# Attention products of a cached decode kernel in four column tiles: V as the moving operand, the sums folded by one fp32 product

## The chip, the cores and the metric

The kernel runs on one core of a Trainium2 chip. The metric is the device time of one execution in microseconds. TensorE (PE) multiplies, with its weight loads shown separately (PEld); VectorE (DVE), ScalarE (ACT) and GpSimd (POOL) do the rest of the arithmetic; SyncE (SP) issues the data transfers, which 16 DMA engines carry out.

## The reference

Eight sequences decode one token each through two identical layers. A layer is layer norm, attention over a cache of 8192 keys with 32 query heads sharing 8 key/value heads, a residual, layer norm, a SiLU feed-forward of width 1792, and a residual. Both layers read the same caches and the same weights.

```
def _A_ref(x, k_cache, v_cache, wq, wo):       # x [8, 1, 512]
    q = (x @ wq).reshape(B, Sq, 32, 128).transpose(0, 2, 1, 3)
    k = jnp.repeat(k_cache, 4, axis=1)         # caches [8, 8, 8192, 128], bf16
    v = jnp.repeat(v_cache, 4, axis=1)
    p = softmax(einsum("bhqd,bhkd->bhqk", q, k) * 128 ** -0.5)
    o = einsum("bhqk,bhkd->bhqd", p, v)
    return o.transpose(0, 2, 1, 3).reshape(B, Sq, 4096) @ wo

x = x + _A_ref(layernorm(x), k_cache, v_cache, wq, wo)
x = x + silu(layernorm(x) @ w1) @ w2
(the same two lines once more)
```

K and V of one pair of a sequence and a key/value head are 2 MB each, of all pairs 268 MB.

## The kernel before

**Tasks.** A task is one layer, one sequence b and one key/value head g: its four query heads against 8192 keys and values. There are 128 tasks. `make_tasks` orders them so that the two layers interleave: of each sequence, the keys of the last five heads stay in SBUF after layer 0 ("kept") and serve layer 1 as well, so that the five layer-1 tasks on them load V alone. The other tasks load K and V. In the steady part a round of fifteen tasks per sequence has five tasks of layer 0 whose keys are kept, five that load everything, and five of layer 1 on kept keys.

**Slots and loads.** `ARENA` has 27 slots of 512 KB. A task's K is four slots and its V four slots. `plan_loads` orders all loads by the position at which they are needed and gives each a slot that an earlier load has left; `issue` (L357) has SP issue the transfer after waiting for the last reader of that slot. Loads therefore run ahead only as far as slots come free.

**Positions.** The main loop (L770) runs over positions p, eight to a task. At each odd position `emit_s` multiplies one K slot and `emit_pv` one V slot of a task 14 positions behind (LP). In between come the pieces of the softmax of the task just scored (`soft`: maximum at phase 0, shift and exponential at 2, sum at 4, transposes at 5, reciprocal at 7), pieces of the `chain` (the dense part of a sequence between its layers: output projection, residual, layer norm, feed-forward, query projection) and the part of the output projection of one head group (`add_heads`). 22 positions after a task's first, `emit_norm` (L561) scales its output. Each engine works strictly in the order in which these calls emit its instructions; waits are semaphores that `op` derives from named resources.

**The attention of a task, in TensorE's terms.** A product is a weight load and a matmul. Column tiles are groups of 32 columns of the array whose results land in 32 partitions of PSUM each.
- `emit_t` (L444): DVE transposes a K slot in place in 32x32 blocks of 4-byte words.
- `emit_q` (L463): four products with the selection matrix `pick` (128 columns of weights, 4 moving columns) spread the query into `QSp`; DVE writes it to `QB` at L466.
- `emit_s` (L481): 16 products per K slot, already in four column tiles: 32 columns of `QB` as weights, 128 columns of K moving, four products accumulated in each tile of `SCp`.
- `softmax_max` (L491), `softmax_shift` (L501): the row maxima, spread out on a diagonal, are multiplied by a 128x128 matrix of ones in fp32, which gives every partition all maxima; DVE takes the smallest negated one (L504, L507).
- `softmax_exp` (L511): ScalarE's exponential from `SCp` to `P`; it reads the bank in order and writes with a step of four elements.
- `emit_pt` (L530): four transposes of 128x128 blocks of P by TensorE; DVE copies the used columns to `PT` (L534).
- `emit_pv` (L554): 16 products per V slot over the full array: 128 columns of V as weights, moving the four probability columns, each repeated 12 times (PVN), so that the four heads' outputs accumulate along the 48 columns of `OTp` over all 64 chunks of a task.
- `emit_norm` (L568): DVE multiplies every twelfth column by the reciprocal sum.

Of the kernel before, what the change touches and what calls it, by code (L numbers as in the profile page):

```python
# [27 lines left out]
KB = 512  # L28
QUAD = 32
FAR = 1e38  # L30
PVN = 12
CW = 32
SETTLE = 2

# [174 lines left out]
def _build(ctx, nc, A_x, A_k_cache, A_v_cache, A_wq, A_wo, B_w1, B_w2, out):  # L209
# [39 lines left out]
    def chunk(slot, c):  # L249
        o = slot * SLOT + c * 128  # L250
        return ARENA[:, o:o + 128]
# [19 lines left out]
    assert NGRAN == NQ and NPART * QUAD == DH  # L271
    QB = [sb([128, NPART, QUAD], BF16, "QB") for _ in range(NQB)]
    own_q = sb([128, NQ], FP32, "own_q")
    pick = sb([128, NPART, 128], BF16, "pick")
# [16 lines left out]
    ones = sb([128, 128], FP32, "ones")  # L291
    hm = sb([128, REP], FP32, "hm")
    real = sb([128, 1], FP32, "real")
    far = sb([128, NQ * USED], FP32, "far")
# [72 lines left out]
    with nc.Block() as block:  # L367

        @block.sync
        def _(sync_eng):  # L370
# [12 lines left out]
            for n in range(NQB):  # L383
# [12 lines left out]
            for i in range(NPART):  # L396
                op(dve, lambda i=i: dve.tensor_copy(
                    pick[:, i, :].rearrange("p (a r) -> p a r", a=NQ),
                    ident[:, i // 2 * 2 * QUAD:(i // 2 + 1) * 2 * QUAD].rearrange("p (r e) -> p e r", e=2)[:, i % 2]
                    .unsqueeze(1).to_broadcast([128, NQ, QUAD])),  # L400
                   reads=["ident"], writes=["pick"])
# [51 lines left out]
            def emit_q(ti):  # L453
                layer, b, g = tasks[ti]
                if layer == 0:
                    q, rq = QT1[:, b * HQ + g * REP:b * HQ + (g + 1) * REP], f"QT1_{b}"
                else:
                    q, rq = QT2[b % 2][:, g * REP:(g + 1) * REP], f"QT2_{b % 2}"
                n = ti % NQB
                steps = []  # L460
                for i in range(NPART):
                    at = (n * NPART + i) * REP
                    steps.append(lambda i=i, at=at: pe.matmul(  # L463
                        QSp[:, at:at + REP], pick[:, i, :], q, start=True, stop=True))
                mm_group(steps, reads=["pick", rq], writes=[f"QS{n}"])
                op(dve, lambda: dve.tensor_tensor(  # L466
                    QB[n][:, :, 0:USED].rearrange("p i (r a) -> p i r a", a=NQ),
                    QSp[:, n * NPART * REP:(n + 1) * NPART * REP].rearrange("p (i r) -> p i r", r=REP).unsqueeze(3)
                    .to_broadcast([128, NPART, REP, NQ]),
                    own_q[:, :].unsqueeze(1).unsqueeze(1).to_broadcast([128, NPART, REP, NQ]), ALU.mult),  # L470
                   reads=[f"QS{n}", "own_q"], writes=[f"QB{n}"])

            def emit_s(i):
                ti = i // GPT
                b, g, k, _h = where(i)
                slot = k_slot[(b, g, k)]
                bank, qn = ti % NSCP, ti % NQB
                keys = ARENA[:, slot * SLOT:(slot + 1) * SLOT].rearrange(
                    "p (t x h j e) -> p t h e x j", t=NQ, x=CPB, h=PAIRS, e=2)
                steps = [  # L480
                    lambda n=n, t=t: pe.matmul(  # L481
                        SCp[bank][t * QUAD:(t + 1) * QUAD, k * 128:(k + 1) * 128], QB[qn][:, n, :],
                        keys[:, t, n // 2, n % 2], start=(n == 0), stop=(n == NPART - 1),
                    )
                    for n in range(NPART) for t in range(NQ)
                ]
                mm_group(steps, reads=[r_half(slot, 0), r_half(slot, 1), f"QB{qn}"], writes=[f"SC{bank}"])
# [9 lines left out]

            def softmax_shift(ti):
                ob = ti % 2
                every = OTp[ob][:, 0:NQ * USED]  # L500
                mm_group([lambda: pe.matmul(every, ones[:, :], spread[:, :], start=True, stop=True)],  # L501
                         reads=["ones", "spread"], writes=[f"OT{ob}"])

                op(dve, lambda: dve.scalar_tensor_tensor(  # L504
                    own[:, :], every, real[:, 0:1], far[:, :], op0=ALU.mult, op1=ALU.add),
                   reads=[f"OT{ob}", "real", "far"], writes=["own"])
                op(dve, lambda: dve.tensor_reduce(shift[:, :], own[:, :], AX.X, ALU.min), reads=["own"], writes=["shift"])  # L507

            def softmax_exp(ti):
                bank, st = ti % NSCP, ti % NST  # L510
                op(act, lambda: act.activation(  # L511
                    P[:, :].rearrange("p (x j k) -> p k x j", x=CPB, k=NGRAN),
                    SCp[bank][:, :].rearrange("p (k x j) -> p k x j", k=NGRAN, x=CPB), ACT.Exp, bias=shift[:, 0:1], scale=SM_SCALE, accum_out=rs[st][:, :]),
                   reads=[f"SC{bank}", "shift"], writes=["P", f"rs{st}"])

            def softmax_sum(ti):
# [7 lines left out]
            def emit_pt(ti):  # L524
                pb = ti % NPT
                tb = evacs[0] % NTP
                evacs[0] += 1
                tpv = TPp[tb][:, 0:KB].rearrange("p (c q) -> p c q", q=128)
                steps = [
                    lambda c=c: pe.transpose(tpv[:, c, :], P[:, c * 128:(c + 1) * 128], ident[:, :])  # L530
                    for c in range(CPB)
                ]
                mm_group(steps, reads=["P", "ident"], writes=[f"TP{tb}"])
                op(dve, lambda: dve.tensor_copy(  # L534
                    PT[pb][:, :, :].rearrange("p x (c q) -> p x c q", q=USED),
                    tpv.rearrange("p x (c q) -> p x c q", q=QUAD)[:, :, :, 0:USED]),
                   reads=[f"TP{tb}"], writes=[f"PT{pb}"])
# [5 lines left out]
            def emit_pv(i):  # L543
                ti = i // GPT
                b, g, k, h = where(i)
                slot = v_slot[(b, g, k)]
                ob, pb = ti % 2, ti % NPT
                pv = PT[pb][:, :, :].rearrange("p x (c r k) -> p x c k r", c=NQ, k=NGRAN)
                otp = OTp[ob][:, 0:REP * PVN].rearrange("p (r n) -> p r n", n=PVN)
                steps = []  # L550
                for c in range(GRP):
                    cc = (i % GPT) * GRP + c
                    steps.append(
                        lambda c=c, cc=cc: pe.matmul(  # L554
                            otp, chunk(slot, h * GRP + c), pv[:, cc % CPB, cc // CPB % NQ, k, :].unsqueeze(2).to_broadcast([128, REP, PVN]),
                            start=(cc == 0), stop=(cc == NCH - 1),
                        )
                    )
                mm_group(steps, reads=[r_half(slot, h), f"PT{pb}"], writes=[f"OT{ob}"])

            def emit_norm(ti):  # L561
                layer, b, g = tasks[ti]
                ob, st = ti % 2, ti % NST
                if layer == 0:
                    dst, rd = at1[b % 3][:, g * REP:(g + 1) * REP], f"at1_{b % 3}"
                else:
                    dst, rd = at2[:, g * REP:(g + 1) * REP, b], f"QT1_{b}"
                op(dve, lambda: dve.tensor_tensor(dst, OTp[ob][:, 0:REP * PVN:PVN], rcp[st][:, :], ALU.mult),  # L568
                   reads=[f"OT{ob}", f"rcp{st}"], writes=[rd])

            def ln_stages(xv, rx, n):
# [198 lines left out]
            for p in range(NG + LP + GPT + 1):  # L770
# [25 lines left out]
                done = p - LP - GPT  # L796
                if done >= 0 and done % GPT == 0 and done // GPT < ntask:
                    tj = done // GPT
                    emit_norm(tj)
                    layer, b, _g = tasks[tj]  # L800
                    if layer == 0:
                        heads[b].append(_g)
                    elif b == B - 1:
                        heads[B].append(_g)
                    if layer == 0 and tj == last0[b]:
                        assert not chain and turn[0] == b
                        chain.extend([lambda b=b: add_heads(b)] * (HKV - summed[b]) + chain_of(b))
                        chain_b[0] = b
                        turn[0] = b + 1
# [49 lines left out]
```

## Time and profile before

Three runs: median 1195.72 us (1193.56 to 1196.29).

| of the profiled execution | value |
|---|---|
| its time | 1198.79 us |
| its span, first to last instruction | 1197.1 us |
| TensorE's mean granted clock | 0.663 of full speed |
| chain that ended last, by engine | DMA 40%, PE 31%, DVE 15%, issue 9%, SP's queue 3%, ACT 2% |
| V loads: number, size, median from issue to landing | 512, 512 KB, 10.3 us |
| K loads | 352, 512 KB, 14.5 us |
| PV products L554: matmuls, busy | 8192, 381.1 us |
| score products L481 | 8192, 287.0 us |
| shift products L501 (two rows to one fp32 product) | 256, 75.4 us |
| transposes L530 | 512, 68.8 us |
| query spread L463 | 512, 32.5 us |
| exponential L511: number, mean | 128, 1409 ns |
| key transposes L444 on DVE: number, mean | 352, 1236 ns |

How to read it: a busy time is the union of an engine's instruction spans; the ends of matmuls are modelled, so products that run side by side in column tiles show up in the union, not in the mean of one. The chain follows the end of the program back from step to step; "issue" in it, and in the waits, is time in which an engine waited for nothing that the profile shows. The DMA queue named "instruction" carries program code, the one named "hardware_dynamic" the data.

### The profile page before, as it was taken

To read this page: it belongs to the slowest core of one execution; us is meant where nothing else is said; L and a number is where in the kernel's file an instruction comes from. 1 tells how busy PE (TensorE), PEld (TensorE's weight loads), DVE (VectorE), ACT (ScalarE), POOL (GpSimd) and SP (SyncE) were. 2 spreads that over 40 slices of the span, in tenths; PEclk is the share of its full clock that TensorE was granted. 3 is DMA by queue.
4 is the path that set the end of the run, shared out by engine and by line. 5 is a ranking of instruction groups with operands and counts; after the bars stand their busy time and mean duration, and the time that the engine had idled before them with its cause. 6 is when DMAs were issued, how large, how long until landed. Compare 5 with 4: busy or idle time off the path is not lost.

```text
span 1197.1 us, 46189 instructions
## 1 busy us (share of the span) xinstructions
PE 839.0 (70%) x20984; PEld 673.4 (56%) x20984; DVE 736.1 (61%) x1830; ACT 183.5 (15%) x266; POOL 70.8 (6%) x172
## 2 busy tenths in 40 slices
PE   1636677767776677767777778777776777677785
PEld 1435566556655566556665566556665656555564
DVE  3736763767456673867457763867376755768464
ACT  0101112111111012111111111111111111111111
POOL 0000000000000000000000000000000000000000
PEclk9955568555765577655866586756775587657765
DMA  9999999999999999999999999999999999999994
GB/s 368 385 396 397 399 355 408 407 394 395 393 408 407 368 389 401 408 404 395 389 408 408 388 397 409 407 402 395 393 407 403 399 393 408 407 392 386 402 408 165
DMA packets 131619, 468.06 MB, mean 391 GB/s; under 512 B 13904, under 2 KB 19808, under 8 KB 130912
## 3 DMA queue, kind: packets, MB, share of 16 engines
q1 hardware_dynamic: 131424, 465.12, 99.1%
q8 instruction: 164, 2.69, 0.9%
q14 instruction: 31, 0.25, 0.1%
HBM read 465.05 MB, written 0.01 MB: 388 GB/s over the span
## 4 chain that ended last, share of the span: by engine, by line
DMA 40%; PE 31%; DVE 15%; issue 9%; SPq 3%; ACT 2%; POOL 0%; POOLq 0%; ACTq 0%; DVEq 0%
DMA arena<-in_A_v_cache_dram 37%; PE OTp L554 14%; PE SCp L481 8%; DVE arena L444 7%; SPq L339 3%; DMA arena<-in_A_k_cache_dram 3%; PE MISC L634 3%; PE OTp L501 2%; PE TPp L530 2%; ACT P L511 2%; DVE rowmax L491 1%; DVE PT L534 1%; PE MISC L652 1%; DVE tr L607 1%; DVE spread L493 1%
## 5 line engine op out<-in xcount | busy, mean ns | idle before, releaser
L554 PE MATMUL OTp<-PT,arena 128*128 128x48 bf16 x8192 | 381.1, 205 | 227.6 <-DMA arena<-in_A_v_cache_dram 182.1
L444 DVE STREAM_TRANSPOSE arena<-arena 128x1024 int32<-128x1024 int32 x352 | 434.9, 1236 | 115.9 <-DMA arena<-in_A_k_cache_dram 115.2
L554 PEld LDWEIGHTS OTp<-PT,arena 128*128 128x128 bf16 x8192 | 316.9, 110 | 331.5 <-DMA arena<-in_A_v_cache_dram 242.6
L511 ACT ACTIVATE P<-SCp,shift 128x512 bf16<-128x512 f32 x128 | 180.3, 1409 | 930.6 <-DVE shift L507 651.5
L481 PE MATMUL SCp<-arena,QB 128*32 128x128 bf16 x8192 | 287.0, 275 | 37.3 <-issue 29.0
L481 PEld LDWEIGHTS SCp<-arena,QB 128*32 128x32 bf16 x8192 | 161.4, 115 | 84.1 <-issue 48.6
L521 POOL PARTITION_ALL_REDUCE ssa<-ssm x128 | 55.6, 435 | 996.0 <-DVE ssm L518 970.8
L534 DVE COPY PT<-TPp 128x256 bf16<-128x256 bf16 x128 | 37.3, 291 | 103.6 <-PE TPp L530 101.8
L501 PE MATMUL OTp<-spread,ones 128*128 128x64 f32 x256 | 75.4, 389 | 25.9 <-DVE spread L493 22.7
L491 DVE TENSOR_REDUCE rowmax<-SCp 128x1 f32<-128x512 f32 x128 | 84.8, 663 | 11.5 <-PE SCp L481 10.3
L530 PE MATMUL TPp<-ident,P 128*128 128x128 bf16 x512 | 68.8, 278 | 13.7 <-ACT P L511 9.6
L504 DVE SCALAR_TENSOR_TENSOR own<-OTp,real,far 128x64 f32<-128x64 f32 x128 | 32.9, 257 | 71.7 <-PE OTp L501 71.7
L501 PEld LDWEIGHTS OTp<-spread,ones 128*128 128x128 f32 x256 | 54.9, 266 | 35.6 <-DVE spread L493 34.4
L518 DVE TENSOR_SCALAR ssm<-hm,rs 128x4 f32<-128x4 f32 x128 | 26.8, 210 | 73.9 <-ACT P L511 73.9
L530 PEld LDWEIGHTS TPp<-ident,P 128*128 128x128 bf16 x512 | 41.7, 122 | 16.5 <-ACT P L511 12.3
L634 PE MATMUL MISC<-xnT,wq 128*128 128x32 bf16 (+1 forms) x1152 | 37.1, 185 | 19.3 <-DVE xnT L621 13.1
L634 PEld LDWEIGHTS MISC<-xnT,wq 128*128 128x128 bf16 x1152 | 35.8, 105 | 20.4 <-issue 16.3
L652 PE MATMUL MISC<-at,wo 128*128 128x32 bf16 x1024 | 37.7, 185 | 6.1 <-issue 4.4
L652 PEld LDWEIGHTS MISC<-at,wo 128*128 128x128 bf16 x1024 | 33.2, 103 | 6.9 <-issue 4.6
L463 PE MATMUL QSp<-QT,pick 128*128 128x4 bf16 x512 | 32.5, 168 | 5.7 <-DVE QT L717 2.9
L493 DVE TENSOR_SCALAR spread<-ident,rowmax 128x64 f32<-128x64 bf16 x128 | 32.6, 255 | 4.5
L511 ACT ACTIVATION_READ_ACCUMULATOR P<-SCp,shift 128x1 f32 x128 | 33.3, 260 | 0.0
(54 smaller groups left out, 276.3 us busy)
## 6 DMA issues: line engine op xcount, KB each, us to landing
arena<-in_A_v_cache_dram SPq DMA_DIRECT2D x512, 512.0 KB, 10.3
arena<-in_A_k_cache_dram SPq DMA_DIRECT2D x352, 512.0 KB, 14.5
wq<-in_A_wq_dram SPq DMA_DIRECT2D x1, 4096.0 KB, 16.6
wo<-in_A_wo_dram SPq DMA_DIRECT2D x1, 4096.0 KB, 26.3
w<-in_B_w_dram SPq DMA_DIRECT2D x2, 1792.0 KB, 22.8
P<-in_A_x_dram SPq DMA_DIRECT2D x1, 8.0 KB
out_dram<-P SPq DMA_DIRECT2D x1, 8.0 KB
```

What stands on the lines that cost most here:

```text
L444: op(dve, lambda: dve.transpose(words, words), reads=[r_half(slot, 0), r_half(slot, 1)], writes=[r_half(slot, 0), r_half(slot, 1)])
L481: lambda n=n, t=t: pe.matmul(SCp[bank][t * QUAD:(t + 1) * QUAD, k * 128:(k + 1) * 128], QB[qn][:, n, :], keys[:, t, n // 2, n % 2], start= ...
L491: op(dve, lambda: dve.tensor_reduce(rowmax[:, :], SCp[bank][:, :], AX.X, ALU.max), reads=[f"SC{bank}"], writes=["rowmax"])
L493: op(dve, lambda: dve.tensor_scalar(spread[:, :].rearrange("p (c q) -> p c q", q=USED), lanes, rowmax[:, 0:1], -SM_SCALE, op0=ALU.mult, op ...
L501: mm_group([lambda: pe.matmul(every, ones[:, :], spread[:, :], start=True, stop=True)], reads=["ones", "spread"], writes=[f"OT{ob}"])
L511: op(act, lambda: act.activation(P[:, :].rearrange("p (x j k) -> p k x j", x=CPB, k=NGRAN), SCp[bank][:, :].rearrange("p (k x j) -> p k x ...
L521: op(pool, lambda: pool.partition_all_reduce(ssa[st][:, :], ssm[st][:, :], 128, bass.bass_isa.ReduceOp.add), reads=[f"ssm{st}"], writes=[f ...
L530: lambda c=c: pe.transpose(tpv[:, c, :], P[:, c * 128:(c + 1) * 128], ident[:, :])
L534: op(dve, lambda: dve.tensor_copy(PT[pb][:, :, :].rearrange("p x (c q) -> p x c q", q=USED), tpv.rearrange("p x (c q) -> p x c q", q=QUAD) ...
L554: lambda c=c, cc=cc: pe.matmul(otp, chunk(slot, h * GRP + c), pv[:, cc % CPB, cc // CPB % NQ, k, :].unsqueeze(2).to_broadcast([128, REP, P ...
L634: lambda o=o, k=k: pe.matmul(MISC[:, o * n:o * n + w], w_sb[:, k, o * 128:(o + 1) * 128], rhs_of(k).to_broadcast([128, w]) if n == 1 else ...
L652: lambda o=o, h=h: pe.matmul(MISC[:, o * w:(o + 1) * w], wo_sb[:, h, o * 128:(o + 1) * 128], rhs_of(h).to_broadcast([128, w]) if n == 1 el ...
```

## The change

All the attention products of a task go to four column tiles.
- PV: the four probability columns become the weights (a product loads 4 columns) and a chunk of V moves (128 columns). Chunk cc goes to tile cc mod 4, so a task's output is four partial sums of [4 heads x 128], one in each group of 32 partitions of `OTp`, columns 0 to 127.
- Fold, new: `emit_fold` has ScalarE copy the four partial sums to `OS` in SBUF; four fp32 products, one per tile, with 32 columns of `OS` as weights and the new [128 x 4] `pick` moving add them and turn them so that the head dimension lies on partitions. They land in four further columns of the `OTp` bank, from which `emit_norm` reads.
- Query spread, shift product and transposes: each product of 128 weight columns becomes four of 32. The query spread takes its selection straight from `ident`; `ones` is [128 x 32].
- Scores: the columns of `SCp` are written four 4-byte words apart, in the order that P needs; the exponential then reads and writes in order.
- At the start the unused rows of `OTp` are set to zero, since the copy and the fold read them too.

The loads, their order, the slots, the key transposes, the dense part and the positions are as before, with the fold emitted just ahead of the norm.

```diff
@@ emit_q
                 for i in range(NPART):
                     at = (n * NPART + i) * REP
-                    steps.append(lambda i=i, at=at: pe.matmul(
-                        QSp[:, at:at + REP], pick[:, i, :], q, start=True, stop=True))
+                    pairs = ident[:, i // 2 * 2 * QUAD:(i // 2 + 1) * 2 * QUAD].rearrange("p (r e) -> p e r", e=2)[:, i % 2]
+                    for a in range(NQ):
+                        steps.append(lambda a=a, at=at, pairs=pairs: pe.matmul(
+                            QSp[a * QUAD:(a + 1) * QUAD, at:at + REP], pairs, q, start=True, stop=True))
@@ emit_s
-                        SCp[bank][t * QUAD:(t + 1) * QUAD, k * 128:(k + 1) * 128], QB[qn][:, n, :],
+                        SCp[bank][t * QUAD:(t + 1) * QUAD, :].rearrange("p (x j k) -> p k x j", x=CPB, k=NGRAN)[:, k], QB[qn][:, n, :],
                         keys[:, t, n // 2, n % 2], start=(n == 0), stop=(n == NPART - 1),
@@ softmax_shift
-                every = OTp[ob][:, 0:NQ * USED]
-                mm_group([lambda: pe.matmul(every, ones[:, :], spread[:, :], start=True, stop=True)],
+                every = OTp[ob][:, DH:DH + NQ * USED]
+                mm_group([lambda t=t: pe.matmul(every[t * QUAD:(t + 1) * QUAD, :], ones[:, :], spread[:, :], start=True, stop=True)
+                          for t in range(NQ)],
@@ softmax_exp
-                    P[:, :].rearrange("p (x j k) -> p k x j", x=CPB, k=NGRAN),
-                    SCp[bank][:, :].rearrange("p (k x j) -> p k x j", k=NGRAN, x=CPB), ACT.Exp, bias=shift[:, 0:1], scale=SM_SCALE, accum_out=rs[st][:, :]),
+                    P[:, :], SCp[bank][:, :], ACT.Exp, bias=shift[:, 0:1], scale=SM_SCALE, accum_out=rs[st][:, :]),
@@ emit_pt
-                    lambda c=c: pe.transpose(tpv[:, c, :], P[:, c * 128:(c + 1) * 128], ident[:, :])
-                    for c in range(CPB)
+                    lambda c=c, k=k: pe.transpose(
+                        tpv[k * QUAD:(k + 1) * QUAD, c, :], P[:, c * 128 + k * QUAD:c * 128 + (k + 1) * QUAD], ident[:, :])
+                    for c in range(CPB) for k in range(NGRAN)
@@ emit_pv
-                otp = OTp[ob][:, 0:REP * PVN].rearrange("p (r n) -> p r n", n=PVN)
                 for c in range(GRP):
                     cc = (i % GPT) * GRP + c
+                    t = cc % NQ
                     steps.append(
-                        lambda c=c, cc=cc: pe.matmul(
-                            otp, chunk(slot, h * GRP + c), pv[:, cc % CPB, cc // CPB % NQ, k, :].unsqueeze(2).to_broadcast([128, REP, PVN]),
-                            start=(cc == 0), stop=(cc == NCH - 1),
+                        lambda c=c, cc=cc, t=t: pe.matmul(
+                            OTp[ob][t * QUAD:t * QUAD + REP, 0:DH], pv[:, cc % CPB, cc // CPB % NQ, k, :], chunk(slot, h * GRP + c),
+                            start=(cc < NQ), stop=(cc >= NCH - NQ),
@@ new
+            def emit_fold(ti):
+                ob = ti % 2
+                op(act, lambda: act.copy(OS[:, :], OTp[ob][:, 0:DH]), reads=[f"OT{ob}"], writes=["OS"])
+                folded = OTp[ob][:, DH + NQ * USED:DH + NQ * USED + REP]
+                mm_group([lambda t=t: pe.matmul(folded[t * QUAD:(t + 1) * QUAD, :], OS[:, t * QUAD:(t + 1) * QUAD], pick[:, :],
+                                                start=True, stop=True) for t in range(NQ)],
+                         reads=["OS", "pick"], writes=[f"OT{ob}"])
@@ emit_norm
-                op(dve, lambda: dve.tensor_tensor(dst, OTp[ob][:, 0:REP * PVN:PVN], rcp[st][:, :], ALU.mult),
+                op(dve, lambda: dve.tensor_tensor(dst, OTp[ob][:, DH + NQ * USED:DH + NQ * USED + REP], rcp[st][:, :], ALU.mult),
@@ main loop
                     tj = done // GPT
+                    emit_fold(tj)
                     emit_norm(tj)
```

More of the change, by code (lines that the diff above doesn't have):

```diff
@@ L30 @@
 FAR = 1e38
-PVN = 12
 CW = 32
@@ L273, in _build @@
     own_q = sb([128, NQ], FP32, "own_q")
-    pick = sb([128, NPART, 128], BF16, "pick")
     at1 = [sb([128, HQ], BF16, "at1") for _ in range(3)]
@@ L290, in _build @@
     PT = [sb([128, CPB, NQ * USED], BF16, "PT") for _ in range(NPT)]
-    ones = sb([128, 128], FP32, "ones")
+    ones = sb([128, QUAD], FP32, "ones")
+    pick = sb([128, REP], FP32, "pick")
+    OS = sb([128, DH], FP32, "OS")
     hm = sb([128, REP], FP32, "hm")
@@ L395, in _ @@
                reads=["ident"], writes=["own_q"])
[L396 to L401, printed above, removed]
+            op(dve, lambda: dve.tensor_reduce(
+                pick[:, :], ident[:, :].rearrange("p (c q) -> p q c", q=QUAD)[:, 0:REP, :], AX.X, ALU.add),
+               reads=["ident"], writes=["pick"])
+            for n in range(2):
+                op(dve, lambda n=n: dve.memset(OTp[n][:, 0:DH], 0.0), writes=[f"OT{n}"])
             for c in range(NQ):
@@ L462, in emit_q @@
                     at = (n * NPART + i) * REP
-                    steps.append(lambda i=i, at=at: pe.matmul(
-                        QSp[:, at:at + REP], pick[:, i, :], q, start=True, stop=True))
-                mm_group(steps, reads=["pick", rq], writes=[f"QS{n}"])
+                    pairs = ident[:, i // 2 * 2 * QUAD:(i // 2 + 1) * 2 * QUAD].rearrange("p (r e) -> p e r", e=2)[:, i % 2]
+                    for a in range(NQ):
+                        steps.append(lambda a=a, at=at, pairs=pairs: pe.matmul(
+                            QSp[a * QUAD:(a + 1) * QUAD, at:at + REP], pairs, q, start=True, stop=True))
+                mm_group(steps, reads=["ident", rq], writes=[f"QS{n}"])
                 op(dve, lambda: dve.tensor_tensor(
```

## The prediction

> **What bounds the kernel now.** I read the page first: span, engines, DMA queues.
>
> ```profile
> span 1197.1 us, 46189 instructions
> PE 839.0 (70%) x20984; PEld 673.4 (56%) x20984; DVE 736.1 (61%) x1830; ACT 183.5 (15%) x266; POOL 70.8 (6%) x172
> ...
> GB/s 368 385 396 397 399 355 408 407 394 395 393 408 407 368 389 401 408 404 395 389 408 408 388 397 409 407 402 395 393 407 403 399 393 408 407 392 386 402 408 165
> ...
> q1 hardware_dynamic: 131424, 465.12, 99.1%
> q8 instruction: 164, 2.69, 0.9%
> ```
>
> 465 MB at the 408 GB/s of the best slices is 1140 us, so the loads fill nearly the whole span, and whoever speeds up an engine gains only where the DMA runs below 408. The last line is the one to notice: 164 packets of 16 KB (2.69 MB / 164) bring instructions. TensorE has 2 x 20984 = 41968 instructions, and 41968 / 164 = 256 each: these packets are TensorE's program.
>
> Next the waits, TensorE's part:
>
> ```profile
> PE OTp L554 <- DMA arena<-in_A_v_cache_dram: 182.1, 198, 16.6
> PE OTp L554 <- issue: 34.6, 25, 2.8
> PE SCp L481 <- issue: 29.0, 25, 2.5
> ```
>
> TensorE waits 182 us for V, and 64 us on these two lines (78 us with the smaller ones) for "issue": for nothing the profile names. The timeline shows such a wait, in the middle of a group of score products whose data is there:
>
> ```profile
> 200.94 0.41 PE L481 MATMUL SCp<-arena,QB 128*32 128x128 bf16 x15
> ...
> 203.23 0.22 PE L481 MATMUL SCp<-arena,QB 128*32 128x128 bf16 x1 [1.88 <-issue]
> ```
>
> The next such waits end at 209.52 and 215.80, the two before at 190.91 and 197.03. The table of stretches between these ends (columns: stretch, length, PE, PEld, DVE, ACT, POOL with counts, clock, DMA share, GB/s), followed by the two parts of one round and by a stretch with a thin data queue:
>
> ```profile
> 190.90:197.02 6.12, 5.09 (x127) 4.11 (x128) 2.17 (x9) 1.41 (x2) 0.43 (x1) 0.72 1.03 406
> 197.02:203.22 6.20, 3.97 (x128) 3.13 (x128) 1.37 (x7) 1.41 (x2) 0.43 (x1) 1.00 1.03 407
> 203.22:209.51 6.29, 5.20 (x128) 3.96 (x127) 3.18 (x9) 1.41 (x2) 0.43 (x1) 0.73 1.02 405
> 209.51:215.80 6.29, 4.86 (x127) 3.87 (x128) 5.21 (x12) 1.42 (x2) 0.43 (x1) 0.69 1.03 410
> ...
> 302.90:369.90 67.00, 52.23 (x1373) 42.20 (x1373) 37.45 (x100) 12.71 (x18) 3.91 (x9) 0.73 1.02 402
> 369.90:435.70 65.80, 44.47 (x1068) 35.73 (x1068) 46.35 (x112) 8.62 (x13) 4.18 (x10) 0.58 1.01 389
> 440.00:450.00 10.00, 8.44 (x254) 7.16 (x255) 3.47 (x11) 1.87 (x3) 0.44 (x1) 0.80 0.91 342
> ```
>
> In the first four TensorE executes 255 or 256 instructions, one packet, and each takes 6.1 to 6.3 us, at clock 1.00 and at 0.69 alike. So **one block of 256 TensorE instructions cannot follow the last in less than about 6.2 us while the DMA is full**, however fast its products are. In the last row, at 342 GB/s, 509 instructions take 10 us: 5.0 us a block. The round trip shortens when the data queue thins.
>
> The kernel runs in rounds of fifteen tasks. The fifth and sixth rows of the table are one, cut at the task ends (L568). The first 9 tasks (five of layer 1 on kept keys, which load V alone, then layer-0 tasks for which loads have run ahead) take 67.0 us for 2746 TensorE instructions: 10.73 blocks of 6.25 us, the fetch limit. The other 6 take 65.8 us for 2136: 8.34 blocks of 7.9 us, and there TensorE waits for data. By bytes the round needs 402 x 67.0 + 389 x 65.8 = 52.5 MB, 128.8 us at 408 GB/s, of 132.8. The hidden resource is not TensorE's busy time but its **count of instructions**.
>
> **The change, part by part.** Counts per task, from the rows of 128 tasks; each product is one MATMUL and one LDWEIGHTS row.
> - Transposes L530: x512 is 4 a task; 16 after: +12. Query spread L463: x512, 4 to 16: +12. Shift product L501: x256 is 2 rows (one fp32 product has two); four products: +6. Fold, new: four fp32 products, by the same two rows +8. Scores and PV keep their 64 each.
> - Sum: +38 products, +76 instructions a task, 276 to 352 without output projection and chain. In all 128 x 76 = 9728 more: 51,696, or 202 blocks for 164.
>
> **Execution time of these parts.** PV: its group of 16 took 0.82 us at clock 0.50 and 0.57 at 1.00; new, it has the form of a score group (128 columns in four tiles), which took 0.62 and 0.42: -0.6 to -0.8 us a task for four groups. Before many PV groups stands a 0.20 us "issue" wait after the scores; if it is the change of tile form, up to -0.8 more. Transposes: 0.60 and 0.38 before, as a score group after: nothing. Query spread: 0.26 for four, between 0.26 and 0.62 for sixteen. Shift: 0.69 for one; between that (side by side) and 4 x 0.69. Fold: between 0.26 (the query row, also of 4 columns) and 4 x 0.69. The sum goes from -1.3 to +4.6 us a task; I take -0.5, because the score rows show tiles side by side at 0.62 / 16 = 39 ns each. In the fetch-bound tasks this counts for nothing either way up to the limit: execution of a fetched block took 6.2 less its wait, 3.5 to 5.3 us, and the rest is the fetch wait that hides it. In the data-bound ones waits for data hide it.
>
> ScalarE: the exponential (L511, 1.41 us) now writes in order. From L682 (184 ns for 14 columns, 265 for 112: 0.83 ns a column) 512 columns would take an estimated 0.60 us. ScalarE is idle 85%; the transposes waited for it 9.6 us in all, so at most that. The new copy to OS (128 columns, by L682 about 0.28 us) is queued after the task's last PV; behind it on ScalarE stand the next exponential and the chain's. TensorE has transposes and an output projection queued before the fold (0.38 to 0.60 each), which cover the copy; uncovered it is 0.4 us a task. The norm (L568) then waits for the fold, and queued behind it on DVE are key transposes (L444): up to 1 us late, in a queue 61% busy and two positions ahead. I take nothing; the upper end allows 0.4 us x 9 fetch-bound tasks a round. Two memsets and a smaller pick at the start: nothing, TensorE idles there from 58 to 74 us for V.
>
> Scores written four words apart: the page has no strided write by TensorE. Lower end nothing; upper end the ratio of the strided exponential to its estimate, 1.41 / 0.60 = 2.35 (of a 0.62 group: +0.84 us, 3.4 a task). I take nothing (a different engine's write), and keep the rest as a rival. [...]
>
> **The fetch, summed.** Loads: 38 packets more. The 164 held 0.9% of 16 engines' span, 10.8 us; 38 take 2.5 us, about 0.3 a round.
> Fetch-bound tasks of a round: 2746 + 9 x 76 = 3430 instructions, 13.4 blocks. At 6.25 us they take 83.7 (+16.7); at the 6.0 us that another block took with a queue five or fewer deep (148.85 to 154.86, 403 GB/s) 80.4. Data-bound tasks: 2136 + 6 x 76 = 2592, 10.1 blocks; at 6.0 they need 60.8, at 5.0 (the thin row) 50.5, and the data hold them as now unless loads have run ahead. They will have: 80.4 us at 402 GB/s bring 32.3 MB where these tasks used 26.9, so about 5.4 MB, 13 us, limited by the 27 slots.
> Upper end: all 23.5 blocks at 6.2: 145.7, +13 a round. Lower end: all at 5.0, 118, under the data's 128.8: +0. Between: a TensorE at its fetch limit frees slots later, the queue thins, the round trip shortens. I take the fetch-bound tasks at 6.0 (80.4) and the data-bound ones at 5.75, three quarters of the way from 5.0 to 6.0 because the DMA must still carry over 370 GB/s (58.1): 138.5, **+5.7 a round**. Seven rounds lie between 169 and 1106 us: +40.
> The end has no data-bound tasks to give time back: 1105.8 to 1182.9, ten tasks, 2936 instructions, 77.1 us, 6.7 a block. +760 instructions are 3.0 blocks: 15 to 18 us, less the 5 us by which 77.1 exceeds 11.5 x 6.25: +12. Before 169 us tasks come 10.2 us apart and their 1.4 to 1.5 blocks take 9: +0. The final fold on the last task's path: +1.
> Sum: the profiled execution took 1198.8 us (span 1197.1 and 1.7 around it); + 40 + 12 + 1 = 1252, and the runs' median lies 3.1 under that execution: **1249 us**.
>
> [...]
>
> **Rivals.**
> 1. *The fetch hides itself.* The thin-queue row's 5.0 us a block times 202 blocks is 1010 us, well inside the span. For: that row. Against: it held for 10 us while the DMA was starved, so it pays in data rate. Time: 1195.7 + 2.5 for packets, up to + 12 for the end: 1198 to 1215. [...]
> 2. *TensorE gets slower to execute than to fetch.* A fetch-bound task executes in at most 276 / 256 x 5.3 = 5.7 us now. Strided scores +3.4 and fp32 products in a row +1.5 (a third of the most) make 10.6, where its fetch takes 80.4 / 9 = 8.9: 1.7 x 9 = 15 us a round beyond mine, 7 rounds: 1354; half of it 1302. For: fp32 and strided forms are unseen. Against: tiles ran side by side in the scores.
> 3. *Faster.* From 160 to 170 us the DMA fell to 287 GB/s while the query chain held TensorE (8.9 us busy): 3 us lost, and about as much at each round's turn. If the cheaper PV groups and saved form changes free slots sooner there, half of 7 x 4 us returns, less 2.5: 1184. It decides only if blocks can be fetched well ahead; against it are equal block times at clocks 1.00 and 0.69.
>
> **From this to the numbers.** Forecast 0.66 (its own range 1215 to 1295), rival 1 0.12, rival 2 0.14, rival 3 0.08. A change under 0.2%, 2.4 us, cannot be told from none here: of rival 1, 0.05 lies inside, the rest is slower. Faster 0.08, same 0.05, slower 0.66 + 0.14 + 0.07 = 0.87. Range 1202 to 1296: nearly all of the forecast, most of rival 1, the mildest of rival 2.
>
> **What would show it.** Instruction packets near 202 and TensorE rows near 2 x 25,850. TensorE's "issue" waits grown from 78 us to 200 or more, its waits for V down from 182. Stretches of 255 or 256 instructions still at 6 us or more. Mean GB/s near 372. PV groups near 0.42 and 0.62; score groups too, else rival 2. I am wrong if blocks come at 5 us while the DMA keeps 400 GB/s, or if the score groups lengthen.

## The result, and the profile after

Four runs of each kernel: before 1196.01 us median (1193.56 to 1196.39), changed 1258.24 us (1255.3 to 1261.39). The ratio is 1.0525, 95% interval 1.049 to 1.0561: slower. The profiled execution of the changed kernel took 1260.67 us, at a mean clock of 0.732 (0.663 before).

The first lines of the changed kernel's page, and its DMA issues:

```profile
span 1258.9 us, 56153 instructions
PE 810.1 (64%) x25848; PEld 663.2 (53%) x25848; DVE 735.6 (58%) x1829; ACT 135.4 (11%) x394; POOL 70.7 (6%) x172
...
GB/s 366 385 398 398 389 331 408 407 336 381 353 407 372 385 339 408 408 356 371 385 407 339 385 341 408 389 366 387 399 407 341 376 363 408 363 365 379 408 408 70
...
q8 instruction: 202, 3.31, 1.1%
...
arena<-in_A_v_cache_dram SPq DMA_DIRECT2D x512, 512.0 KB, 8.8
arena<-in_A_k_cache_dram SPq DMA_DIRECT2D x352, 512.0 KB, 9.3
```

TensorE is busy for less time than before (810.1 us for 839.0), in a longer span. The packets that bring its program are 202 for 164. The data rate falls to 331 to 341 GB/s in six slices, about one a round, where the lowest two had been 355 and 368. And a K load lands 9.3 us after its issue (the median), where it took 14.5. SP's waits for PV and the scores to leave a slot, on its wait line (L91, in the change L90), grew from 443 to 583 us: slots come free later; that a queue thinner for it shortens the landing is a reading.

TensorE's waits (in all, how often, longest):

```profile
PE OTp L556 <- DMA arena<-in_A_v_cache_dram: 96.6, 96, 13.3
PE SCp L482 <- issue: 84.0, 46, 3.5
PE OTp L556 <- issue: 80.3, 46, 3.4
...
PE TPp L531 <- issue: 23.3, 12, 3.5
```

With the smaller lines, "issue" has grown from 79 to 246 us and the waits for V have shrunk from 182 to 97. The timeline has such waits in the middle of groups, as before:

```profile
202.26 0.60 PE L482 MATMUL SCp<-arena,QB 128*32 128x128 bf16 x14
202.61 0.48 PE L556 MATMUL OTp<-arena,PT 128*4 128x128 bf16 x16
...
203.45 0.24 PE L567 MATMUL OTp<-pick,OS 128*32 128x4 f32 x8
...
203.93 0.44 PE L556 MATMUL OTp<-arena,PT 128*4 128x128 bf16 x16
204.19 0.49 PE L482 MATMUL SCp<-arena,QB 128*32 128x128 bf16 x9
208.09 0.61 PE L482 MATMUL SCp<-arena,QB 128*32 128x128 bf16 x7 [3.41 <-issue]
...
209.07 1.13 PE L482 MATMUL SCp<-arena,QB 128*32 128x128 bf16 x15
```

A score group stops after 9 of its 16 products and waits 3.41 us for nothing that the profile names. The stretches between the ends of such waits, then the round of the prediction cut at the same two tasks (its first nine, its other six) and the last eleven tasks; columns as in the prediction (length, PE, PEld, DVE, ACT, POOL with counts, clock, DMA share, GB/s):

```profile
195.58:201.94 6.36, 4.98 (x129) 4.38 (x128) 2.17 (x8) 1.04 (x3) 0.43 (x1) 0.56 1.03 408
201.94:208.09 6.15, 2.60 (x127) 2.15 (x128) 1.71 (x6) 0.27 (x1) 0.00 (x0) 0.99 1.03 408
208.09:214.29 6.20, 4.09 (x129) 3.86 (x129) 1.15 (x5) 1.05 (x3) 0.43 (x1) 0.74 1.03 408
...
312.40:391.60 79.20, 51.39 (x1728) 45.69 (x1728) 37.92 (x99) 9.40 (x27) 3.90 (x9) 0.78 0.99 384
391.60:451.50 59.90, 40.89 (x1284) 31.51 (x1288) 45.78 (x114) 6.34 (x19) 4.18 (x10) 0.73 0.98 364
1160.40:1244.90 84.50, 57.83 (x1832) 49.02 (x1832) 39.28 (x106) 10.52 (x31) 4.32 (x10) 0.70 0.88 347
```

The first three are 255 to 258 instructions each. At clock 0.99 they execute in 2.60 us and at 0.56 in 4.98, and both times the next block begins after 6.2 to 6.4 us. The nine tasks take 79.2 us where they took 67.0; the six take 59.9 where they took 65.8: they give part of it back.

The groups whose form the change altered (busy, mean ns of one):

```profile
L482 PE MATMUL SCp<-arena,QB 128*32 128x128 bf16 x8192 | 461.0, 394 | 92.7 <-issue 84.0
...
L556 PE MATMUL OTp<-arena,PT 128*4 128x128 bf16 x8192 | 314.5, 280 | 179.2 <-DMA arena<-in_A_v_cache_dram 96.6
...
L513 ACT ACTIVATE P<-SCp,shift 128x512 bf16<-128x512 f32 x128 | 88.0, 687 | 807.4 <-DVE shift L509 449.7
...
L565 ACT COPY OS<-OTp 128x128 f32<-128x128 f32 x128 | 34.0, 266 | 233.2 <-PE OTp L556 233.1
```

PV is cheaper (314.5 us for 381.1, at a mean clock of 0.732 for 0.663), the exponential half as long (687 ns for 1409), but the scores are dearer: 461.0 us for 287.0. That is new, and has to be told apart from the fetch.

### The profile page after: what moved, and what is told of

Same layout as the page of the kernel before. It is cut to its first block, busy times and chain, and to the rows that moved or that the text cites. A ratio compares the mean times of both kernels' runs of the same rounds, so it can differ in the third digit from the quotient of the medians.

```text
span 1258.9 us, 56153 instructions
## 1 busy us (share of the span) xinstructions
PE 810.1 (64%) x25848; PEld 663.2 (53%) x25848; DVE 735.6 (58%) x1829; ACT 135.4 (11%) x394; POOL 70.7 (6%) x172
## 5 line engine op out<-in xcount | busy, mean ns | idle before, releaser
L482 PE MATMUL SCp<-arena,QB 128*32 128x128 bf16 x8192 | 461.0, 394 | 92.7 <-issue 84.0
L556 PE MATMUL OTp<-arena,PT 128*4 128x128 bf16 x8192 | 314.5, 280 | 179.2 <-DMA arena<-in_A_v_cache_dram 96.6
L556 PEld LDWEIGHTS OTp<-arena,PT 128*4 128x4 bf16 x8192 | 240.8, 125 | 239.0 <-DMA arena<-in_A_v_cache_dram 143.2
L482 PEld LDWEIGHTS SCp<-arena,QB 128*32 128x32 bf16 x8192 | 268.7, 146 | 113.0 <-issue 96.4
L513 ACT ACTIVATE P<-SCp,shift 128x512 bf16<-128x512 f32 x128 | 88.0, 687 | 807.4 <-DVE shift L509 449.7
L531 PE MATMUL TPp<-ident,P 128*32 128x128 bf16 x2048 | 71.6, 263 | 28.3 <-issue 23.3
L502 PE MATMUL OTp<-spread,ones 128*32 128x64 f32 x1024 | 54.1, 279 | 31.6 <-DVE spread L494 24.0
L531 PEld LDWEIGHTS TPp<-ident,P 128*32 128x32 bf16 x2048 | 50.3, 120 | 34.2 <-issue 26.0
L464 PE MATMUL QSp<-QT,ident 128*32 128x4 bf16 x2048 | 41.7, 172 | 20.3 <-issue 17.4
L464 PEld LDWEIGHTS QSp<-QT,ident 128*32 128x32 bf16 x2048 | 38.2, 110 | 23.0 <-issue 19.3
```

Source lines behind the costliest of these rows:

```text
L464: steps.append(lambda a=a, at=at, pairs=pairs: pe.matmul(QSp[a * QUAD:(a + 1) * QUAD, at:at + REP], pairs, q, start=True, stop=True))
L482: lambda n=n, t=t: pe.matmul(SCp[bank][t * QUAD:(t + 1) * QUAD, :].rearrange("p (x j k) -> p k x j", x=CPB, k=NGRAN)[:, k], QB[qn][:, n, : ...
L502: mm_group([lambda t=t: pe.matmul(every[t * QUAD:(t + 1) * QUAD, :], ones[:, :], spread[:, :], start=True, stop=True) for t in range(NQ)], ...
L513: op(act, lambda: act.activation(P[:, :], SCp[bank][:, :], ACT.Exp, bias=shift[:, 0:1], scale=SM_SCALE, accum_out=rs[st][:, :]), reads=[f" ...
L531: lambda c=c, k=k: pe.transpose(tpv[k * QUAD:(k + 1) * QUAD, c, :], P[:, c * 128 + k * QUAD:c * 128 + (k + 1) * QUAD], ident[:, :])
L556: lambda c=c, cc=cc, t=t: pe.matmul(OTp[ob][t * QUAD:t * QUAD + REP, 0:DH], pv[:, cc % CPB, cc // CPB % NQ, k, :], chunk(slot, h * GRP + c ...
```

## The experiments

Two theories stand against each other. F, the prediction's: the count of TensorE's instructions sets the time, since a block of 256 cannot follow the last in less than about 6.2 us while the DMA is full (6.12 to 6.29 us in the four of the prediction). X: the strided score writes, 174 us more busy time, set it. The table has all runs; "issue" and "V" are TensorE's waits for nothing that is named and for data, in us over all lines of the profile of each. Each ratio is to runs of the kernel before made alongside; their medians lie between 1194.84 and 1196.01 us.

| run | what it is | packets | median us | ratio to before, 95% | GB/s | issue | V |
|---|---|---|---|---|---|---|---|
| before | | 164 | 1196.01 | | 391 | 79 | 182 |
| the change | | 202 | 1258.24 | 1.0525 (1.0490 to 1.0561) | 372 | 246 | 97 |
| count38 | before + 38 products a task | 202 | 1270.23 | 1.0603 (1.0569 to 1.0638) | 371 | 134 | 75 |
| count19 | before + 19 | 183 | 1217.31 | 1.0185 (1.0155 to 1.0215) | 385 | 78 | 102 |
| scores_plain | change, scores in order | 202 | 1256.01 | 1.0496 (1.0462 to 1.0530) | 374 | 269 | 113 |
| strided_only | before, strided scores | 164 | 1197.09 | 1.0001 (0.9985 to 1.0017) | 392 | 75 | 147 |
| full_width | change, spread and transposes whole | 178 | 1210.64 | 1.0123 (1.0079 to 1.0166) | 388 | 156 | 124 |
| pv_only | the same, scores in order | 178 | 1206.35 | 1.0102 (1.0065 to 1.0139) | 389 | 157 | 175 |
| wide_pv | PV 512 columns at a time | 120 | 1188.77 | 0.9940 (0.9912 to 0.9968) | 394 | 3 | 251 |
| wide_strided | wide_pv, strided scores | 120 | 1192.32 | 0.9978 (0.9964 to 0.9991) | 393 | 2 | 145 |
| wide_count38 | wide_pv + 38 | 158 | 1199.52 | 1.0039 (1.0025 to 1.0054) | 391 | 39 | 154 |
| wide_count82 | wide_pv + 82, in two clumps | 202 | 1297.33 | 1.0859 (1.0815 to 1.0902) | 363 | 152 | 60 |
| wide_count82s | wide_pv + 82, spread, bank shared | 202 | 1313.70 | 1.0992 (1.0966 to 1.1017) | 357 | 51 | 27 |
| wide_count82t | wide_pv + 82, spread | 202 | 1269.90 | 1.0629 (1.0579 to 1.0680) | 370 | 153 | 70 |

**The count alone.** The kernel before, with 38 small products a task whose results nobody reads: 20 ahead of the query spread and 18 ahead of the shift product. This gives the change's instruction count and nothing else of it, except that the added products have to be executed.

```diff
@@ emit_q (softmax_shift has range(18), into OTp[ob] columns 256:260)
+                steps = [
+                    lambda a=a: pe.matmul(QSp[a % NQ * QUAD:(a % NQ + 1) * QUAD, 64:64 + REP], ident[:, 0:QUAD], ident[:, 0:REP],
+                                          start=True, stop=True)
+                    for a in range(20)
+                ] + steps
```

> The kernel before with 38 small products a task added (32 weight columns, 4 moving columns, results unused; 20 ahead of the query spread, 18 ahead of the shift product): 51,696 TensorE instructions, 202 blocks, as many as the changed kernel has, and nothing else of the change. Theory F (the fetch of TensorE's instructions sets the loss): 1240 to 1265 us, instruction packets 202, 'issue' waits of TensorE over 180 us, scores still at 0.42 and 0.62 us a group. Rival X (the execution of the strided scores sets it): 1196 to 1206, since 38 products at some 25 to 50 ns are 1 to 2 us a task beside other work.

TensorE's waits in its profile:

```profile
PE OTp L564 <- DMA arena<-in_A_v_cache_dram: 75.2, 93, 12.5
PE OTp L564 <- issue: 47.3, 37, 2.8
PE SCp L486 <- issue: 45.4, 34, 2.9
```

1270.23 us: the whole loss of the change and 12 us more, with plain scores, PV over the full array and no fold. It is 5 us above what F expected, so something adds to the count; TensorE is busy for 943 us here, 810 in the change. F also missed the waits for "issue": over 180 us expected, 134 measured. That fits the longer execution, since what a block executes longer it waits less, and over the seven steady rounds the packets come 5.96 us apart in the mean, in the change 5.95. Half the products (10 and 9 in the same places):

> The kernel before with 19 small unused products a task instead of 38: 46,832 TensorE instructions, 183 blocks. F with a loss in proportion to the count (38 gave 1270): 1232. F with a cover (the tasks that wait for data take up the first blocks): 1212 to 1224.

183 packets gave 1217.31 us. The first 19 packets cost 1.85%, the next 19 about 4.2% (6.03 less 1.85): the price of a packet rises as the tasks that waited for data run out of slack (waits for V 182, 102, 75 us). That is F with a cover; in proportion to the count it would have been 1232.

**The scores.** The change with the scores written in order and the exponential striding, as before:

```diff
@@ emit_s, after
-                        SCp[bank][t * QUAD:(t + 1) * QUAD, :].rearrange("p (x j k) -> p k x j", x=CPB, k=NGRAN)[:, k], QB[qn][:, n, :],
+                        SCp[bank][t * QUAD:(t + 1) * QUAD, k * 128:(k + 1) * 128], QB[qn][:, n, :],
```

> The changed kernel with the scores written in order again and the exponential writing with its step; instruction count unchanged. F: 1243 to 1262 us, the score groups back at 0.42 and 0.62 us, the exponential back at 1.41. X: under 1215.

The reverse, the strided scores and the exponential in order in the kernel before, all else as it was:

> The kernel before with the scores written four words apart and the exponential in order, nothing else: 41,968 TensorE instructions as before. F: 1190 to 1203 us, although the score groups take 0.62 and some 1.1 us. X: over 1230.

The PV and score groups of this second kernel, before with strided scores:

```profile
L553 PE MATMUL OTp<-PT,arena 128*128 128x48 bf16 x8192 | 343.9, 195 | 191.4 <-DMA arena<-in_A_v_cache_dram 147.0
...
L481 PE MATMUL SCp<-arena,QB 128*32 128x128 bf16 x8192 | 401.4, 362 | 36.8 <-issue 28.8
```

The strided write does lengthen the scores, by 114 us of busy time (401.4 for 287.0), but the time doesn't move: 1.0001. Two things take up most of it. The waits for V fall from 182 to 147 us, and PV is busy 37 us less (343.9 for 381.1), at a mean clock of 0.787 for 0.663. The waits for "issue" stay at 75. Taken out of the change, the strided scores give back 0.3 of 5.25%, which the intervals don't tell from nothing. X falls.

**Which products.** The change with the query spread and the transposes over the full array again (4 products each instead of 16); PV, shift and fold stay tiled. That is 24 products a task less, 178 packets.

```diff
@@ emit_pt, after
-                    lambda c=c, k=k: pe.transpose(
-                        tpv[k * QUAD:(k + 1) * QUAD, c, :], P[:, c * 128 + k * QUAD:c * 128 + (k + 1) * QUAD], ident[:, :])
-                    for c in range(CPB) for k in range(NGRAN)
+                    lambda c=c: pe.transpose(tpv[:, c, :], P[:, c * 128:(c + 1) * 128], ident[:, :])
+                    for c in range(CPB)
@@ emit_q: one product over 128 columns per part in place of four over 32
```

> The changed kernel with the transposes and the query spread at full width again (4 products each), PV in tiles, fold, shift in tiles and strided scores kept: 304 TensorE instructions a task, 45,552, 178 blocks. F: 1203 to 1225. If PV in tiles or the fold itself costs (their execution, the waits for ScalarE's copy): over 1235.

And the same with the scores in order:

> The same with the scores written in order as well, so of the change PV in tiles, the fold and the shift in tiles remain: 178 blocks. F: within 0.6% of the run with strided scores beside it, 1200 to 1225. If the strided scores cost once the fetch leaves room: some 5 us or more below it.

1210.64 and 1206.35 us, both within F's ranges and 0.4% apart: three quarters of the loss (4.0 of 5.25%) go with the 24 products that only split what had been whole, the last 24 of the packets' steep range. What stays, 14 products a task, costs 1.0 to 1.2%.

**Fewer instructions than before.** If the count is what binds, V should move in larger pieces. In this kernel a PV product moves 512 columns, four chunks of V, and its weights are 16 columns (four chunks by four heads). Only the results where a chunk meets its own probabilities are used. The fold is four bf16 products over a copy, one position later than in the change; it and the shift product write to the `QSp` bank. 16 PV products a task stand for 64, 120 packets for 164.

```diff
@@ emit_pv, before
-                            otp, chunk(slot, h * GRP + c), pv[:, cc % CPB, cc // CPB % NQ, k, :].unsqueeze(2).to_broadcast([128, REP, PVN]),
-                            start=(cc == 0), stop=(cc == NCH - 1),
+                            OTp[ob][t * QUAD:t * QUAD + CPB * REP, :], pv[:, w % NQ, k, :],
+                            half(slot, h)[:, s * CPB * 128:(s + 1) * CPB * 128],
+                            start=(w < NQ), stop=(w >= NCH // CPB - NQ),
@@ new, emit_take
+                op(act, lambda: act.copy(OS[:, :], OTp[ob][:, :]), reads=[f"OT{ob}"], writes=["P"])
...
@@ new, emit_fold
+                mm_group([lambda x=x: pe.matmul(QSp[:, 96:96 + REP], OS[:, x * DH:(x + 1) * DH], pick[:, x * REP:(x + 1) * REP],
+                                                start=(x == 0), stop=(x == CPB - 1)) for x in range(CPB)],
+                         reads=["P", "pick"], writes=["fold", "QSB"])
```

> PV with V moving, but in products of 512 columns of V and 16 probability columns as weights (four chunks by four heads, of which the diagonal blocks count), four tiles, folded by four bf16 products; transposes, query spread, shift and scores as before: 188 TensorE instructions a task for 276 before and 352 after, 30,704 in all, 120 blocks. F: block limit out of the way, 1165 to 1188 us, 'issue' waits under 20 us, data rate over 395 GB/s. X: TensorE's execution is no shorter than in the kernel before by much (streaming of V is the same as in the change), 1190 to 1205.

The wide kernel's page and waits, and one round's nine and six tasks:

```profile
GB/s 359 387 395 408 402 354 410 408 405 395 385 408 409 394 397 408 409 407 393 400 408 409 399 399 408 408 407 397 405 407 408 401 398 408 409 400 371 406 408 158
...
q8 instruction: 120, 1.97, 0.7%
```

```profile
PE OTp L563 <- DMA arena<-in_A_v_cache_dram: 250.8, 293, 17.7
...
PE SCp L490 <- issue: 2.5, 4, 0.9
```

```profile
301.30:368.60 67.30, 49.94 (x990) 28.00 (x990) 38.46 (x99) 17.98 (x27) 3.89 (x9) 0.65 1.02 399
368.60:432.80 64.20, 43.59 (x792) 24.71 (x796) 46.63 (x113) 12.06 (x19) 4.16 (x10) 0.53 1.02 400
```

The waits for "issue" are gone (3.0 us), and TensorE waits for V instead: the data bind in both parts, 399 and 400 GB/s where the kernel before had 402 and 389. 1188.77 us, 0.6% under before, is the best of all these versions. It lies 0.8 us above F's range and 1.2 us under X's, and the rate of 394 GB/s over the span just misses F's 395. The waits for "issue" decide for F; with the fetch out of the way the loads are what is left.

Strided scores in this kernel, where no fetch hides them:

> The kernel with PV in products of 512 columns (120 blocks), with the scores strided and the exponential in order as in the change. With no fetch limit to hide in, longer score groups (some +0.5 us each at clock 0.5) show if they matter: over 1194. If the data alone bound it: 1183 to 1192, with a shorter exponential at the end.

0.4% dearer than wide_pv, with intervals that just touch. At 1192.32 us it falls between the two forecasts (up to 1192, over 1194) and settles neither. Then 38 small products a task back in, in the places of the first experiment, now in the `QSp` bank:

> The kernel with PV in 512-column products plus the same 38 small unused products a task (20 ahead of the query spread, 18 ahead of the shift): 40,432 TensorE instructions, 158 blocks, fewer than the kernel before has. F: within 0.6% of that kernel without them, 1186 to 1198, although the same 38 cost 74 us in the kernel before. If the small products cost by their execution or by the waits of their groups: over 1220.

158 packets, about as many as before: 1199.52 us, about as before. That is a narrow miss: F had up to 1198 and 0.6% above wide_pv, and the ratios put it 1.0% above. So 38 packets cost 1.0% from 120 up, where the same 38 cost 6.0% from 164 up.

**The same count by another way.** With 82 small products a task (42 and 40) the wide kernel has the change's 202 packets:

> The same with 82 small products a task: 51,696 TensorE instructions, 202 blocks, as many as the changed kernel. F: 1245 to 1275 whatever PV looks like, 'issue' waits back over 130 us. If the count matters only together with PV of 64 products a task: under 1215.

1297.33 us, 39 above the change: a miss. Either the clumps did it, or TensorE's busy time, 938 us. A first try to spread them put 16 ahead of each score group:

> The same 82 small products a task as the run at 1297 us, but spread: 16 ahead of each of the four score groups and 18 ahead of the shift, instead of 42 and 40 in two places. 202 blocks. If the 27 to 40 us by which that run passed the change at the same count came from the uneven filling of the blocks (blocks of quick small products run into the fetch limit, the others into their execution): 1250 to 1275. If they come from 512-column PV beside a full fetch: 1285 to 1305 again.

1313.70 us, but inconclusive: they wrote to the bank of the query spread, and had to wait for DVE's reads of it. Two of its waits:

```profile
PE QSp L502 <- DVE QB L480: 123.4, 128, 3.8
PE QSp L502 <- DVE own L528: 64.7, 110, 2.0
```

That is 188 us on two lines that the clumped version lacks. The last run writes 64 of them into the score columns that the scores then overwrite; the 18 ahead of the shift product stay in `QSp`:

```diff
@@ emit_s, wide_pv
+                more = [
+                    lambda a=a: pe.matmul(SCp[bank][a % NQ * QUAD:(a % NQ + 1) * QUAD, k * 128:k * 128 + REP], ident[:, 0:QUAD], ident[:, 0:REP],
+                                          start=True, stop=True)
+                    for a in range(16)
+                ]
```

> The wide-PV kernel with the same 82 small unused products a task as before, spread out: 16 ahead of each of a task's four score groups, into the columns of the score bank that the scores then overwrite (so no bank is shared with a reader that was not there already, and no wait is added on DVE), and 18 ahead of the shift product. 202 instruction packets again, as in the change. With 42 and 40 of them in two clumps a task the time was 1297 us against 1258 of the change at the same count. If the 39 us came from the clumps (a block full of small products ends early and waits for its successor, the next one is full of long products and takes longer than its fetch), the spread ones give 1245 to 1270 us, TensorE's waits for nothing near 200 us. If what counts is TensorE's busy time on top of the count (about 940 us in the clumped run, 810 in the change), it stays at 1285 to 1305 us.

1269.90 us, at the upper end of its forecast: 27 of the 39 us went when the clumps were spread. (The bank of 64 products changed with that, but the clumped version waits only 1.7 us ahead of the query spread for the shift product's reader on DVE.) The waits for "issue" were 153 us where some 200 were expected. The other 12 us stay, as in count38 (1270.23), the other kernel at 202 packets with TensorE busy for over 900 us (914 here). What makes these 12 us was not tried further; that both have the longer busy time is all that the runs show.

**Busy time against count, over all runs.** wide_strided keeps TensorE busy for 922 us with 120 packets and takes 1192 us; scores_plain keeps it busy for 725 us with 202 packets and takes 1256. So busy time alone doesn't set the time. The traces also show where TensorE stops. Its instructions, with the few of its sequencer, can be counted off in blocks of 256. Of the change's 190 pauses of over 1 us from the start of one instruction to the next, 121 fall on one and the same of the 256 places, and no other place has more than three. On that place the kernel before has 45 of 177 pauses, strided_only 45, full_width 76, scores_plain 117, count38 82, wide_pv and wide_strided one each.

## Why the prediction was right

Forecast 1249 us, measured 1258.24; the profiled execution, to which the sum was made, 1252 forecast and 1260.67 measured.

- **The mechanism holds.** Blocks of 255 to 258 instructions at 6.15 to 6.36 us with the DMA at 408 GB/s; 202 packets and 25,848 products (202 and 25,850 forecast); "issue" 246 us (200 or more); 372 GB/s (near 372). The count alone gives the whole loss, fewer instructions than before remove the wait. That the size came out so close is in part luck, since errors offset each other: the rounds were 11.9 us dearer than forecast and the start 2.6, the end 4.6 cheaper.
- **The round, +5.7.** The first nine tasks were to take 80.4 us and took 79.2; over six rounds cut alike they took 79.6 in the mean (67.8 before). The other six were to take 58.1 and took 59.9 here, 60.0 in the mean (64.5 before). The mis-sized term is the second: 10.1 blocks were given 5.75 us and took 5.94 in the mean. The fetch alone doesn't set that: in the round shown these six tasks still hold 9.7 us of waits for V beside 5.5 for "issue", where the nine have 21.8 for "issue" and none for V. The seven rounds from 178.1 to 1105.9 us before now reach from 180.7 to 1160.4: +51.9, 7.4 a round, where +40 was forecast.
- **The end, +12.** Eleven tasks (the prediction counted ten in the same stretch, and began its seven rounds one task early; together that is under 2 us) took 84.5 us for 77.1, +7.4: their 3664 instructions are 14.3 blocks at 5.9 us. The forecast of 89 had them at over 6.1, the rate of a full queue, and here the data ran at 347 GB/s. At the start +2.6 for +0. After the last norm nothing for +1. In sum 51.9 + 7.4 + 2.6 - 0.1 = 61.8, the difference of the spans, for a forecast of 53.
- **Execution, nothing.** A PV group takes 0.44 to 0.48 us at full clock (0.42 forecast). The fp32 products of shift and fold do run side by side (eight rows of the fold in 0.24 us), the copy takes 266 ns (280), the exponential 687 (600). The strided scores were taken at nothing and cost much: about 0.62 us a group instead of 0.42 at full clock, 1.13 for 15 products at a slow one instead of 0.62 a group. The prediction had named longer score groups as a sign of being wrong. They came, and the forecast stood: the cover, fetch waits and data waits, was there (0.3% between the change and scores_plain), and that sign was chosen wrongly.
- **Rival 1** (the fetch hides itself) is out: the mean of 5.95 us from packet to packet over the seven rounds is above the thin-queue row's 5.0. Of all versions only wide_pv and wide_strided have next to no waits for "issue" (3 and 2 us); their packets come over 9 us apart in the mean. **Rival 2** had a true premise, the dearer scores, but not its consequence: a block of the new scores still executes in 2.6 to 5.0 us, under its fetch. **Rival 3** had its cheaper PV groups, and in the slices at about the rounds' turns the data rate fell to 331 to 341 GB/s rather than rose (its sum also took 4 us a turn where its own row gives 3).

## What to carry to other kernels

Count an engine's instructions against the time in which its program can be fetched: when stalls that the profile puts down to nothing recur after the same number of instructions, whatever the clock (here after 255 to 258, 6.15 to 6.36 us apart at clocks of 0.56 to 0.99), splitting a product into column tiles adds to that count, however fast the tiles run (here 38 more products a task, 202 packets for 164, cost 62 us; one block of the change executed in 2.60 us and still took 6.15). Before making products cheaper, ask whether fewer and larger ones do the work: 16 products of 512 columns in place of 64 of 128 took 1.0 to 0.994, 64 smaller tiles and their helpers to 1.0525. A stall of one part can be paid back in another that waits for data (here nine tasks took 79.2 us for 67.0, the next six 59.9 for 65.8); the price per instruction is low while there is such slack (1.0% for 38 packets from 120) and rises steeply after it (4.2% for the last 19 of 202).

## What the runs showed of the hardware

- **In these traces one block of the program was fetched ahead, and no more.** By the packets in the change's trace, a block begins at 201.94 us; the packet of the next one starts at 205.56 and lands at 206.67, and its first instruction runs at 208.09. That is 3.6 us to the packet's start, 1.1 for 16 KB, 1.4 until it is used, and the packet starts 3.6 to 3.8 us after the block at all ten such stalls from 189 to 251 us. Over the change's whole trace exactly one packet starts between the first instructions of any two successive blocks, and in that of the kernel before, so none was fetched further ahead there. That the 3.6 us are spent behind queued data is a reading; blocks of 5.0 us at 342 GB/s in the kernel before fit it.
- **The score products took longer when they wrote to PSUM with a stride.** Four words apart, the mean score product went from 275 to 362 ns in the kernel before (strided_only), and its busy time by 40% (401.4 for 287.0 us), though the mean clock was higher (0.787 for 0.663).
- **The granted clock rose with the strided scores**, though TensorE was then busy for longer. Over all runs of each, the mean clock was 0.641 to 0.666 before (beside strided_only) and 0.776 to 0.805 with strided scores; 0.605 to 0.661 in scores_plain and 0.731 to 0.739 in the change; 0.641 to 0.652 in pv_only and 0.734 to 0.740 in full_width. In the wide kernel it rose little: 0.624 to 0.669, then 0.670 to 0.681. No run here says why.
